# The opening loads of a fused attention and MLP kernel are regrouped, and its first input chunk is turned into eight half banks

## The chip, the cores and the metric

The kernel runs on one core of a Trainium2 chip. A core has a matrix engine (TensorE, PE in the profile), a vector engine (VectorE, DVE), an activation engine (ScalarE, ACT), a general engine (GpSimd, POOL) and SyncE (SP), which here only issues transfers. Each works through its own list of instructions in order, and waits on semaphores that other engines or transfers raise. Sixteen DMA engines move data between the device memory and the core's SBUF. Matrix products land in PSUM, which has eight banks of 128 partitions by 512 fp32 values.

The metric is device time in microseconds (us), lower is better. The kernel before takes 155.68 us, the median of three runs (155.62 to 155.93).

## The reference: what is computed

Inputs and output are bfloat16; `x` is 2048 by 512.

```python
x = A_x                                   # (1, 2048, 512)
g = sigmoid((x * gate_w).sum(-1, keepdims=True))
q, k, v = split heads of x @ wqkv         # 32 heads of 16
pq, pk = q @ w_phi[h], k @ w_phi[h]       # per head, 16 by 16
phi = concat(softmax(p), softmax(-p))     # 32 features, for q and for k
kv, z = phi_k^T v, sum of phi_k           # per head
o = (phi_q kv) / (phi_q z + 1e-6)
a = o @ wo
b = relu(x @ w1) @ w2                     # 512 -> 1376 -> 512
out = g * a + (1 - g) * b
```

## The kernel before, in words

**How the work is ordered.** Every piece of work is a task with a name, an engine, a list of tasks it depends on, an assumed duration and an assumed latency (`add`, lines 45 to 55). `schedule` (lines 94 to 121) places the tasks in time by a priority, tries random changes of the priorities, and keeps the order with the shortest plan; `emit` (lines 133 to 146) then writes each engine's list in that order, with a wait wherever a dependency crosses engines. So a change in a dependency or in an assumed number can move instructions on every engine.

**The opening.** All first loads are issued at once from two queues, SP and ACT (lines 287 to 295), with two small ones from POOL. `x0a` and `x0b` are the two halves of the first 512 rows of `x`; `wka` and `wkb` are the halves of the key weights; `w1a`, `w1b0`, `w1b1` and `w1c` are pieces of W1 and `wv` the value weights. While they are under way, TensorE runs eight dummy products (`warm`, line 262). Then, in this order:

- `xt`: the first chunk of `x` is turned by products with the identity, sixteen of 128 by 128 (line 342), into four PSUM banks; `xe` copies the turned chunk to SBUF, two copies on ACT (line 354) and two on DVE (line 357), each 128 by 512.
- `h0_0`, `h0_1`: the first two of eleven column tiles of `x @ w1` for chunk 0, four products each (line 397). Tile k of W1 covers columns 128k to 128k+127. `rl` is the ReLU behind each, on ACT.
- `wt`: the key weights are turned the same way (line 328) and copied out by `we`.
- `f1`: `w_phi` is folded into the key weights (line 372) and copied out by `fe1`. `f0` is the same for the query weights.
- `pr_k0` to `pr_k8`, `pr_q0` to `pr_q8`: the projections of two row tiles of 128 each (the last two of one) with the folded weights (line 468).
- `v0` to `v15`: the values of one row tile (line 448), copied out by `ve` on ACT; all of them use PSUM bank 2.

The other three chunks of `x` and the query weights come in through transposing transfers on the SP queue (lines 301 to 304). The first of them, `x1`, waits for `w1b1`, and the loads of W2 and Wo stand behind them on the same queue.

**The softmax chain.** For each projection J: `ev` (ACT) copies it to SBUF, `mx` and `mn` (DVE, lines 500 and 502) take the maximum and minimum of each head, `t1` and `t2` (POOL, line 509) subtract, `ex` (ACT, line 516) exponentiates, `sm` and `rc` (DVE) sum and invert, and `nm` (POOL, lines 525 and 548) scales. For the keys, `kv` (PE, line 532) then accumulates over all rows. For the queries, `tq` (SP, line 551) is a transposing transfer of one row tile, `nd` (PE, line 575) makes numerator and denominator in two halves, `rd` and `o` (DVE) divide, `to` (SP, line 588) is a transposing transfer of the result, and `a` (PE, line 602) multiplies it by Wo on top of `b` (PE, line 596), the eleven products with W2. `oe` (ACT) scales the sum and `st` stores it. All `tq` and `to` go through the one SP queue, in the planned order.

**The folds of the query weights.** `SP0` says behind which chunk of `h` the four folds `f0` stand in the chain that shares the PSUM banks 3, 4 and 5: with -1 behind chunk 1.

Of the kernel before, what the change touches and what calls it, by code (L numbers as in the profile page):

```python
# [6 lines left out]
ACT = mybir.ActivationFunctionType  # L7
# [141 lines left out]
def bass_gated_mix__linear_kernel_hedgehog__dense_activation_relu__prompt_kernel(  # L149
# [30 lines left out]
    NPB, NTS, NF, NSL = 3, 3, 4, 3  # L180
    NPH, NOM, NOT, NOS = 6, 3, 4, 4
    GATE_LIMIT = 40.0
    NWARM = 8
    RL = 400.0
    FE = "dve"
    SP0 = -1

    with ExitStack() as es:
        E = es.enter_context
# [4 lines left out]
        XT = sb("XT", [P, ND, S], BF16)  # L194
# [3 lines left out]
        WV = sb("WV", [P, ND, D], BF16)  # L198
        W1 = sb("W1", [P, ND, W1C], BF16)
# [22 lines left out]
        IDN = sb("IDN", [P, P], BF16)  # L222
# [9 lines left out]
        PS = E(nc.psum_tensor("PS", [P, 8, 512], FP32))  # L232
# [54 lines left out]
        load("x0a", "sp", XN[:, 0:2, :], x0r[:, 0:2, :], dur=0.5, lat=3.7)  # L287
        load("x0b", "act", XN[:, 2:4, :], x0r[:, 2:4, :], dur=0.5, lat=3.7)
        load("w1a", "sp", W1[:, :, 0:256], w1r[:, :, 0:256], dur=0.5, lat=5.5)
        load("wka", "act", WK[:, 0:2, :], wkr[:, 0:2, :], dur=0.5, lat=5.0)  # L290
        load("wkb", "sp", WK[:, 2:4, :], wkr[:, 2:4, :], dur=0.5, lat=5.8)
        load("w1b0", "act", W1[:, 0:2, 256:768], w1r[:, 0:2, 256:768], dur=0.5, lat=8.0)
        load("w1b1", "sp", W1[:, 2:4, 256:768], w1r[:, 2:4, 256:768], dur=0.5, lat=8.0)
        load("wv", "act", WV[:, :, :], A_wqkv[:, 2 * D:3 * D].rearrange("(j p) n -> p j n", p=P), dur=0.5, lat=11.1)
        load("w1c", "sp", W1[:, :, 768:DFF], w1r[:, :, 768:DFF], dur=0.5, lat=10.4)
        load("wphi", "pool", WPS[:, :, :], A_w_phi.rearrange("(g hl) r c -> (hl r) g c", g=ND), dur=0.9, lat=5.7)
        load("gw", "pool", W1[:, :, DFF:DFF + 1], gate_w.rearrange("(j p o) -> p j o", p=P, o=1), dur=0.8, lat=8.0,
             allow_slow_non_contiguous=True)
        g.follow("iota_r", "iota_i")
        g.follow("iota_i", "wphi")  # L300
        load_t("x1", XT[:, :, chunk(1)], x2[chunk(1), :], ("w1b1",), 2.6, 2.3)
        load_t("x2", XT[:, :, chunk(2)], x2[chunk(2), :], (), 2.0, 4.3)
        load_t("wqT", WT[:, 0:ND, :], A_wqkv[:, 0:D], (), 3.8, 2.3)
        load_t("x3", XT[:, :, chunk(3)], x2[chunk(3), :], (), 2.1, 2.2)
# [29 lines left out]
            else:  # L334
                add(name, eng, lambda q: q.tensor_copy(out_, PS[:, b, :]), deps, dur=0.69, **how)

        XB, WB, FB = (0, 1, 6, 7), (2, 6, 7, 0), (1, 2, 6, 7)

        def pe_xt(q, p, hf):
            for n in range(4):  # L340
                j, m = 2 * p + n // 2, 2 * hf + n % 2
                last = q.matmul(PS[:, XB[2 * hf + p], n * P:(n + 1) * P], XN[:, m, j * P:(j + 1) * P], IDN[:, :],
                                start=True, stop=True)
            return last

        for hf, ld in enumerate(("x0a", "x0b")):
            half = slice(hf * 256, (hf + 1) * 256)
            for p in range(2):
                add(f"xt{p}{hf}", "pe", lambda q, p=p, hf=hf: pe_xt(q, p, hf), (ld, "ident"), dur=0.32,
                    boost=9000.0 - 10 * (ND * hf + p))  # L350
                o3 = XT[:, 2 * p:2 * p + 2, half]
                i3 = PS[:, XB[2 * hf + p], :].rearrange("p (j t) -> p j t", j=2)
                if p == 0:
                    add(f"xe{p}{hf}", "act", lambda q, o=o3, i=i3: q.activation(o, i, ACT.Copy), (f"xt{p}{hf}",),  # L354
                        dur=0.6, boost=9000.0)
                else:
                    add(f"xe{p}{hf}", "dve", lambda q, o=o3, i=i3: q.tensor_copy(o, i), (f"xt{p}{hf}",), dur=0.69,  # L357
                        boost=9000.0)
        for i in range(ND):
            add(f"wt{i}", "pe", lambda q, i=i: pe_turn(q, WB[i], [WK[:, j, i * P:(i + 1) * P] for j in range(ND)]),  # L360
                ("wka", "wkb", "ident",
                *((f"xe{XB.index(WB[i]) % 2}{XB.index(WB[i]) // 2}",) if WB[i] in XB else ())), dur=0.28, boost=1900.0)
            evict(f"we{i}", ("act", "dve")[i % 2], WT[:, ND + i, :], WB[i], (f"wt{i}",), boost=1900.0)
        x0 = [f"xe{p}{hf}" for p in range(2) for hf in range(2)]
        xof = [x0, ["x1"], ["x2"], ["x3"]]
        wkt = [f"we{i}" for i in range(ND)]

# [78 lines left out]
        def pe_v(q, m):  # L446
            for j in range(ND):
                last = q.matmul(PS[:, 2, :], XT[:, j, m * P:(m + 1) * P], WV[:, j, :],  # L448
                                start=(j == 0), stop=(j == ND - 1))
# [24 lines left out]
        for jn, (kind, tiles) in enumerate(jobs):  # L474
# [15 lines left out]
            def old(x, J2=two):  # L490
# [1 line left out]

            add(f"pr_{J}", "pe", lambda q, s=s, tiles=tiles: pe_proj(q, s, tiles),
                [*(f"fe{s}_{j}" for j in range(ND)), *(d for m in tiles for d in xof[m // 4]),
                 *([f"ev_{before}"] if before else ["fe1_0", "we3"])], dur=0.87 * w)
            add(f"ev_{J}", "act", lambda q, pb=pb, w=w: q.activation(  # L496
                PB[:, pb, 0:w * D], PS[:, 0:w, :].rearrange("p a b -> p (a b)"), ACT.Copy),
                (f"pr_{J}", old("t1"), old("t2"), old("mx"), old("mn")), dur=0.15 + 0.43 * w)
# [11 lines left out]
                    (f"{'mx' if sg == 0 else 'mn'}_{J}", old("ex"), "warm"), dur=0.19 + 0.86 * w)  # L510
            war = [(f"kv{m}" if jobs[jn - NF][0] == "k" else f"tq{m}") for m in jobs[jn - NF][1]] if jn >= NF else []
            if jn == NF - 2:
                war += [f"xt{p}{hf}" for p in range(2) for hf in range(2)]
# [158 lines left out]
```

## Time and profile before

| | us |
|---|---|
| median of three runs | 155.68 |
| the profiled execution | 156.26 |
| its span | 154.5 |
| around the span | 1.8 |
| TensorE busy (936 products) | 147.5, 96% of the span |
| GpSimd busy | 111.1, 72% |
| VectorE busy | 113.8, 74% |
| ScalarE busy | 94.2, 61% |
| first projection `pr_k0` starts | 13.97 |
| first GpSimd subtraction `t1_k0` starts | 18.10 |

The profiled execution is 0.58 us above the median, so differences are read in it and applied to the median. The granted TensorE clock is given as 1.00 throughout. The chain of waits names 56% of the span for TensorE and 29% for GpSimd; both readings come from the same stretch, since between 10.3 and 99 us TensorE hardly rests while GpSimd is nearly as full.

### The profile page before, as it was taken

To read this page: it belongs to the slowest core of one execution; us is meant where nothing else is said; L and a number is where in the kernel's file an instruction comes from. 1 tells how busy PE (TensorE), PEld (TensorE's weight loads), DVE (VectorE), ACT (ScalarE), POOL (GpSimd) and SP (SyncE) were. 2 spreads that over 40 slices of the span, in tenths; PEclk is the share of its full clock that TensorE was granted. 3 is DMA by queue.
4 is the path that set the end of the run, shared out by engine and by line. 5 is a ranking of instruction groups with operands and counts; after the bars stand their busy time and mean duration, and the time that the engine had idled before them with its cause. 6 is when DMAs were issued, how large, how long until landed. Compare 5 with 4: busy or idle time off the path is not lost.

```text
span 154.5 us, 2461 instructions
## 1 busy us (share of the span) xinstructions
PE 147.5 (96%) x936; PEld 72.8 (47%) x936; DVE 113.8 (74%) x168; ACT 94.2 (61%) x127; POOL 111.1 (72%) x73
## 2 busy tenths in 40 slices
PE   6789999999999999999999999799999999999992
PEld 2455444554545644545454545344555445445440
DVE  3353668999986998489999777599789968934310
ACT  2366589969498959898997817386037712511123
POOL 8000396999999999999999999999786639530000
PEclk9999999999999999999999999999999999999999
DMA  4999999501000000000000061927569576697221
GB/s 138 268 345 234 117 240 311 173 1 1 6 0 0 0 5 0 2 0 0 5 0 0 0 136 34 147 63 170 149 157 143 145 192 159 148 162 178 72 68 68
DMA packets 43571, 15.59 MB, mean 101 GB/s; under 512 B 36532, under 2 KB 43556, under 8 KB 43560
## 3 DMA queue, kind: packets, MB, share of 16 engines
q1 hardware_dynamic: 39848, 12.01, 36.5%
q10 hardware_dynamic: 3648, 3.41, 7.6%
q0 software_dynamic: 64, 0.02, 0.4%
q8 instruction: 7, 0.11, 0.4%
q14 instruction: 4, 0.03, 0.1%
HBM read 4.94 MB, written 2.11 MB: 46 GB/s over the span
## 4 chain that ended last, share of the span: by engine, by line
PE 56%; POOL 29%; DMA 8%; issue 3%; ACT 1%; SPq 1%; ACTq 0%
PE PS L596 20%; POOL TS L509 15%; POOL FT L525 11%; PE PS L397 11%; PE PS L468 10%; PE PS L602 8%; DMA W<-in_B_w_dram 5%; PE PS L448 4%; DMA PHQ<-FT 3%; POOL FT L548 2%; PE PS L575 2%; SPq L272 1%; ACT OSB L609 1%; PE PS L532 1%; PE PS L372 1%
## 5 line engine op out<-in xcount | busy, mean ns | idle before, releaser
L397 PE MATMUL PS<-XT,W 128*128 128x512 bf16 (+1 forms) x176 | 41.4, 379 | 1.7 <-DVE XT L357 1.0
L509 POOL TENSOR_TENSOR TS<-PB,MX 128x1024 bf16<-128x1024 bf16 (+1 forms) x18 | 31.0, 1723 | 15.9 <-DVE MX L500 15.9
L518 DVE TENSOR_REDUCE ZB<-FT 128x128 f32<-128x2048 bf16 (+1 forms) x18 | 36.6, 2035 | 5.5 <-ACT FT L516 5.4
L596 PE MATMUL PS<-W,HT 128*128 128x512 bf16 (+1 forms) x176 | 40.6, 379 | 0.0
L516 ACT ACTIVATE FT<-TS 128x2048 bf16<-128x2048 bf16 (+1 forms) x18 | 30.9, 1716 | 11.7 <-POOL TS L509 11.7
L509 POOL TENSOR_TENSOR TS<-MN,PB 128x1024 bf16<-128x1024 bf16 (+1 forms) x18 | 31.0, 1724 | 1.9 <-DVE MN L502 1.9
L468 PE MATMUL PS<-WP,XT 128*128 128x512 bf16 x128 | 30.6, 379 | 0.0
L412 ACT ACTIVATE HT<-PS 128x512 bf16<-128x512 f32 (+1 forms) x44 | 25.9, 596 | 6.4 <-PE PS L397 5.8
L525 POOL TENSOR_TENSOR FT<-FT,SC 128x2048 bf16<-128x2048 bf16 (+1 forms) x9 | 29.5, 3285 | 0.0
L609 ACT ACTIVATE OSB<-PS,OMG 128x512 bf16<-128x512 f32 x16 | 11.0, 686 | 28.8 <-PE PS L602 28.8
L397 PEld LDWEIGHTS PS<-XT,W 128*128 128x128 bf16 (+1 forms) x176 | 17.2, 100 | 20.7 <-ACT XT L354 1.1
L596 PEld LDWEIGHTS PS<-W,HT 128*128 128x128 bf16 (+1 forms) x176 | 16.3, 98 | 17.7 <-ACT OSB L609 0.2
L500 DVE TENSOR_REDUCE MX<-PB 128x64 bf16<-128x1024 bf16 (+1 forms) x18 | 19.2, 1068 | 6.1 <-ACT PB L496 6.1
L502 DVE TENSOR_REDUCE MN<-PB 128x64 bf16<-128x1024 bf16 (+1 forms) x18 | 19.5, 1082 | 0.0
L496 ACT ACTIVATE PB<-PS 128x1024 bf16<-128x1024 f32 (+1 forms) x18 | 16.6, 923 | 4.6 <-PE PS L468 4.2
L468 PEld LDWEIGHTS PS<-WP,XT 128*128 128x128 bf16 x128 | 12.2, 98 | 13.9
L581 DVE RECIPROCAL RD<-PS 128x16 f32<-128x16 f32 x32 | 6.9, 239 | 14.3 <-PE PS L575 14.2
L448 PE MATMUL PS<-WV,XT 128*128 128x512 bf16 x64 | 16.4, 379 | 0.0
L602 PE MATMUL PS<-WO,OT 128*128 128x512 bf16 x64 | 16.1, 378 | 0.0
L548 POOL TENSOR_TENSOR FT<-FT,SR 128x1024 bf16<-128x1024 bf16 (+1 forms) x9 | 15.7, 1739 | 0.5
L583 DVE SCALAR_TENSOR_TENSOR OTM<-PS,EG,RD 128x256 bf16<-128x256 f32 x32 | 14.1, 463 | 0.1
L457 ACT ACTIVATE VS<-PS 128x512 bf16<-128x512 f32 x16 | 9.5, 595 | 2.6 <-PE PS L448 2.6
(47 smaller groups left out, 87.9 us busy)
## 6 DMA issues: line engine op xcount, KB each, us to landing
out_dram<-OSB ACTq DMA_DIRECT2D x16, 128.0 KB, 1.7
W<-in_B_w_dram SPq DMA_DIRECT2D x1, 1280.0 KB, 7.7
W<-in_B_w_dram SPq DMA_DIRECT2D x1, 608.0 KB, 10.2
W<-in_B_w_dram SPq DMA_DIRECT2D x2, 256.0 KB, 6.6
WV<-in_A_wqkv_dram ACTq DMA_DIRECT2D x1, 512.0 KB, 10.6
WO<-in_A_wo_dram SPq DMA_DIRECT2D x1, 512.0 KB, 7.8
FT<-in_A_x_dram SPq DMA_DIRECT2D x1, 256.0 KB, 3.3
FT<-in_A_x_dram ACTq DMA_DIRECT2D x1, 256.0 KB, 3.6
```

The source lines that it names most:

```text
L397: last = q.matmul(PS[0:m, b, :], W1[:, j, k * P:k * P + m], XT[:, j, chunk(c)], start=(j == 0), stop=(j == ND - 1))
L412: add(f"rl{a}_{k}", "act", lambda q, a=a, k=k, b=b, rows=rows: q.activation(HT[0:rows, k, chunk(a)], PS[0:rows, b, :], ACT.Relu), (prev,), ...
L448: last = q.matmul(PS[:, 2, :], XT[:, j, m * P:(m + 1) * P], WV[:, j, :], start=(j == 0), stop=(j == ND - 1))
L468: last = q.matmul(PS[:, n, :], XT[:, j, m * P:(m + 1) * P], WP[:, s, j, :], start=(j == 0), stop=(j == ND - 1))
L500: add(f"mx_{J}", "dve", lambda q, sl=sl, w=w, i=pbg: q.tensor_reduce(MX[:, sl, 0:w * H], i, AX.X, ALU.max), (f"ev_{J}", old("t1")), dur=0. ...
L502: add(f"mn_{J}", "dve", lambda q, sl=sl, w=w, i=pbg: q.tensor_reduce(MN[:, sl, 0:w * H], i, AX.X, ALU.min), (f"ev_{J}", old("t2")), dur=0. ...
L509: add(f"{tn}_{J}", "pool", lambda q, o3=o3, a3=a3, b3=b3: q.tensor_tensor(o3, a3, b3, ALU.subtract), (f"{'mx' if sg == 0 else 'mn'}_{J}", ...
L516: add(f"ex_{J}", "act", lambda q, fs=fs, ts=ts, w=w: q.activation(FT[:, fs, 0:w * F], TS[:, ts, 0:w * F], ACT.Exp), (f"t1_{J}", f"t2_{J}", ...
L518: add(f"sm_{J}", "dve", lambda q, fs=fs, sl=sl, w=w: q.tensor_reduce(ZB[:, sl, 0:2 * w * H], FT[:, fs, 0:w * F].rearrange("p (g d) -> p g ...
L525: add(f"nm_{J}", "pool", lambda q, f3=f3, sl=sl, w=w: q.tensor_tensor(f3, f3, SC[:, sl, 0:2 * w * H].unsqueeze(2).to_broadcast([P, 2 * w * ...
L596: last = q.matmul(PS[:, ab, :], HT[0:r, k, m * P:(m + 1) * P], W2[0:r, k, :], start=(k == 0), stop=False)
L602: last = q.matmul(PS[:, ab, :], OT[:, m % NOT, t, :], WO[:, t, :], start=False, stop=(t == ND - 1))
```

## The change

The nine first loads become nine others. `x0a` and `x0b` stay. W1's first 512 columns (tiles 0 to 3) come next, as two halves by rows, one on each queue (`w1a0`, `w1a1`), in place of 256 columns on SP. The key weights follow as halves `wk0` and `wk1`. Then come the other 864 columns of W1, again in halves (`w1b0`, `w1b1`), and `wv` last, on SP in place of ACT. The transfer `x1` waits for the new `w1b0`.

The turn of chunk 0 is cut from four groups of four products into eight groups of two, each into the first half of a bank of its own, so that all eight banks are used. There are eight copies of 128 by 256 in place of four of 128 by 512. The banks of `wt`, `f1` and the dependencies that protect them are renamed to match. The dummy products go from eight to seven, and `SP0` from -1 to -2, which puts the four folds `f0` behind chunk 2 of `h`.

The plan that comes out has on TensorE, up to the first projection: seven dummies, sixteen `xt`, `h0_0`, `h0_1`, `wt`, `h0_2`, `h0_3`, `f1`, `v0`, `h0_4`, `pr_k0`. Before, it was: eight dummies, `xt`, `h0_0`, `h0_1`, `wt`, `h0_2`, `f1`, `h0_3`, `h0_4`, `pr_k0`, `v0`. From there to `nd2` the same tasks stand in a somewhat other order on every engine.

```diff
-    NWARM = 8
+    NWARM = 7
-    SP0 = -1
+    SP0 = -2
...
-        load("w1a", "sp", W1[:, :, 0:256], w1r[:, :, 0:256], dur=0.5, lat=5.5)
-        load("wka", "act", WK[:, 0:2, :], wkr[:, 0:2, :], dur=0.5, lat=5.0)
-        load("wkb", "sp", WK[:, 2:4, :], wkr[:, 2:4, :], dur=0.5, lat=5.8)
-        load("w1b0", "act", W1[:, 0:2, 256:768], w1r[:, 0:2, 256:768], dur=0.5, lat=8.0)
-        load("w1b1", "sp", W1[:, 2:4, 256:768], w1r[:, 2:4, 256:768], dur=0.5, lat=8.0)
-        load("wv", "act", WV[:, :, :], A_wqkv[:, 2 * D:3 * D].rearrange("(j p) n -> p j n", p=P), dur=0.5, lat=11.1)
-        load("w1c", "sp", W1[:, :, 768:DFF], w1r[:, :, 768:DFF], dur=0.5, lat=10.4)
+        wvr = A_wqkv[:, 2 * D:3 * D].rearrange("(j p) n -> p j n", p=P)
+        qs = ("sp", "act")
+        for n, q in enumerate(qs):
+            load("x0" + "ab"[n], q, XN[:, 2 * n:2 * n + 2, :], x0r[:, 2 * n:2 * n + 2, :], dur=0.5, lat=3.7)
+        for name, dst, src, lat in (("w1a", W1[:, :, 0:512], w1r[:, :, 0:512], 4.8), ("wk", WK, wkr, 5.9),
+                                    ("w1b", W1[:, :, 512:DFF], w1r[:, :, 512:DFF], 8.0)):
+            for n, q in enumerate(qs):
+                load(f"{name}{n}", q, dst[:, 2 * n:2 * n + 2, :], src[:, 2 * n:2 * n + 2, :], dur=0.5, lat=lat)
+        load("wv", "sp", WV[:, :, :], wvr, dur=0.5, lat=9.0)
...
-        load_t("x1", XT[:, :, chunk(1)], x2[chunk(1), :], ("w1b1",), 2.6, 2.3)
+        load_t("x1", XT[:, :, chunk(1)], x2[chunk(1), :], ("w1b0",), 2.6, 2.3)
...
-        XB, WB, FB = (0, 1, 6, 7), (2, 6, 7, 0), (1, 2, 6, 7)
+        XB, WB, FB = (0, 1, 6, 7, 2, 3, 4, 5), (0, 1, 6, 7), (0, 1, 6, 7)
-        def pe_xt(q, p, hf):
-            for n in range(4):
-                j, m = 2 * p + n // 2, 2 * hf + n % 2
+        def pe_xt(q, j, hf):
+            for n in range(2):
+                last = q.matmul(PS[:, XB[4 * hf + j], n * P:(n + 1) * P], XN[:, 2 * hf + n, j * P:(j + 1) * P],
+                                IDN[:, :], start=True, stop=True)
...
+            for j in range(ND):
+                add(f"xt{j}{hf}", "pe", lambda q, j=j, hf=hf: pe_xt(q, j, hf), (ld, "ident"), dur=0.2,
+                    boost=9000.0 - 10 * (ND * hf + j))
+                xo, xi = XT[:, j, half], PS[:, XB[4 * hf + j], 0:256]
+                if j % 2 == 0:
+                    add(f"xe{j}{hf}", "act", lambda q, o=xo, i=xi: q.activation(o, i, ACT.Copy), (f"xt{j}{hf}",),
+                        dur=0.35, boost=9000.0)
                 else:
+                    add(f"xe{j}{hf}", "dve", lambda q, o=xo, i=xi: q.tensor_copy(o, i), (f"xt{j}{hf}",), dur=0.37,
                         boost=9000.0)
...
-            war = ["xe10"] if j == 0 else [f"we{j - 1}"]
+            war = [f"we{j}"]
...
-        freed = {b: () for b in HB}
-        w1of = {k: (("w1a",) if k < 2 else ("w1b0", "w1b1") if k < 6 else ("w1c",)) for k in range(KT)}
+        freed = {b: (f"xe{XB.index(b) % 4}{XB.index(b) // 4}",) for b in HB}
+        w1of = {k: (("w1a0", "w1a1") if k < 4 else ("w1b0", "w1b1")) for k in range(KT)}
...
-            add(f"v{m}", "pe", lambda q, m=m: pe_v(q, m), (*xof[m // 4], "wv", f"ve{m - 1}" if m else "fe1_1"), dur=0.87)
+            add(f"v{m}", "pe", lambda q, m=m: pe_v(q, m), (*xof[m // 4], "wv", f"ve{m - 1}" if m else "xe01"), dur=0.87)
...
-                 *([f"ev_{before}"] if before else ["fe1_0", "we3"])], dur=0.87 * w)
+                 *([f"ev_{before}"] if before else ["fe1_0", "fe1_1"])], dur=0.87 * w)
```

More of the change, by code (lines that the diff above doesn't have):

```diff
@@ L286, in bass_gated_mix__linear_kernel_hedgehog__dense_activation_relu__prompt_kernel @@
         wkr = A_wqkv[:, D:2 * D].rearrange("(j p) n -> p j n", p=P)
-        load("x0a", "sp", XN[:, 0:2, :], x0r[:, 0:2, :], dur=0.5, lat=3.7)
-        load("x0b", "act", XN[:, 2:4, :], x0r[:, 2:4, :], dur=0.5, lat=3.7)
-        load("w1a", "sp", W1[:, :, 0:256], w1r[:, :, 0:256], dur=0.5, lat=5.5)
-        load("wka", "act", WK[:, 0:2, :], wkr[:, 0:2, :], dur=0.5, lat=5.0)
-        load("wkb", "sp", WK[:, 2:4, :], wkr[:, 2:4, :], dur=0.5, lat=5.8)
-        load("w1b0", "act", W1[:, 0:2, 256:768], w1r[:, 0:2, 256:768], dur=0.5, lat=8.0)
-        load("w1b1", "sp", W1[:, 2:4, 256:768], w1r[:, 2:4, 256:768], dur=0.5, lat=8.0)
-        load("wv", "act", WV[:, :, :], A_wqkv[:, 2 * D:3 * D].rearrange("(j p) n -> p j n", p=P), dur=0.5, lat=11.1)
-        load("w1c", "sp", W1[:, :, 768:DFF], w1r[:, :, 768:DFF], dur=0.5, lat=10.4)
+        wvr = A_wqkv[:, 2 * D:3 * D].rearrange("(j p) n -> p j n", p=P)
[7 more added lines that the diff above has]
+        load("wv", "sp", WV[:, :, :], wvr, dur=0.5, lat=9.0)
         load("wphi", "pool", WPS[:, :, :], A_w_phi.rearrange("(g hl) r c -> (hl r) g c", g=ND), dur=0.9, lat=5.7)
@@ L335, in evict @@
                 add(name, eng, lambda q: q.tensor_copy(out_, PS[:, b, :]), deps, dur=0.69, **how)
-        XB, WB, FB = (0, 1, 6, 7), (2, 6, 7, 0), (1, 2, 6, 7)
-        def pe_xt(q, p, hf):
-            for n in range(4):
-                j, m = 2 * p + n // 2, 2 * hf + n % 2
-                last = q.matmul(PS[:, XB[2 * hf + p], n * P:(n + 1) * P], XN[:, m, j * P:(j + 1) * P], IDN[:, :],
-                                start=True, stop=True)
+        XB, WB, FB = (0, 1, 6, 7, 2, 3, 4, 5), (0, 1, 6, 7), (0, 1, 6, 7)
[3 more added lines that the diff above has]
+                                IDN[:, :], start=True, stop=True)
             return last
@@ L347, in bass_gated_mix__linear_kernel_hedgehog__dense_activation_relu__prompt_kernel @@
             half = slice(hf * 256, (hf + 1) * 256)
[L348 to L355, printed above, removed]
+            for j in range(ND):
[5 more added lines that the diff above has]
+                        dur=0.35, boost=9000.0)
                 else:
-                    add(f"xe{p}{hf}", "dve", lambda q, o=o3, i=i3: q.tensor_copy(o, i), (f"xt{p}{hf}",), dur=0.69,
+                    add(f"xe{j}{hf}", "dve", lambda q, o=xo, i=xi: q.tensor_copy(o, i), (f"xt{j}{hf}",), dur=0.37,
                         boost=9000.0)
@@ L360, in bass_gated_mix__linear_kernel_hedgehog__dense_activation_relu__prompt_kernel @@
             add(f"wt{i}", "pe", lambda q, i=i: pe_turn(q, WB[i], [WK[:, j, i * P:(i + 1) * P] for j in range(ND)]),
-                ("wka", "wkb", "ident",
-                *((f"xe{XB.index(WB[i]) % 2}{XB.index(WB[i]) // 2}",) if WB[i] in XB else ())), dur=0.28, boost=1900.0)
+                ("wk0", "wk1", "ident",
+                f"xe{i}0"), dur=0.28, boost=1900.0)
             evict(f"we{i}", ("act", "dve")[i % 2], WT[:, ND + i, :], WB[i], (f"wt{i}",), boost=1900.0)
-        x0 = [f"xe{p}{hf}" for p in range(2) for hf in range(2)]
+        x0 = [f"xe{j}{hf}" for j in range(ND) for hf in range(2)]
         xof = [x0, ["x1"], ["x2"], ["x3"]]
@@ L512, in bass_gated_mix__linear_kernel_hedgehog__dense_activation_relu__prompt_kernel @@
             if jn == NF - 2:
-                war += [f"xt{p}{hf}" for p in range(2) for hf in range(2)]
+                war += [f"xt{j}{hf}" for j in range(ND) for hf in range(2)]
             if jn == NF - 1:
```

## The prediction

> **What bounds the kernel now.** I read the busy shares first, then the chain of waits in order of time, then the waits, then the landings of the first loads, and last the transfers around the one gap in TensorE's work.
>
> ```profile
> PE 147.5 (96%) x936; PEld 72.8 (47%) x936; DVE 113.8 (74%) x168; ACT 94.2 (61%) x127; POOL 111.1 (72%) x73
> ```
>
> TensorE is the bound: 7.0 us of the span are all it does not fill. The chain says where those are:
>
> ```profile
> 2.30 7.89 DMA W<-in_B_w_dram
> 10.19 0.14 issue
> 10.33 1.02 PE PS L397 x4
> 11.35 0.89 PE PS L372 x16
> 12.24 1.73 PE PS L397 x8
> 13.97 1.73 PE PS L468 x8
> 15.70 0.86 PE PS L448 x4
> ...
> 95.62 4.50 DMA PHQ<-FT
> 100.12 0.05 issue
> 100.16 0.30 PE PS L575 x4
> ```
>
> `w1b1`, issued at 2.30, lands at 10.19 and releases `h0_2`. From there TensorE has no gap until 99.15, where it waits 1.0 us for `tq2`. The waits name the same places:
>
> ```profile
> ACT XT L354 <- PE PS L342: 1.1, 1, 1.1
> ...
> PE PS L575 <- DMA PHQ<-FT: 1.0, 1, 1.0
> PE PS L397 <- DVE XT L357: 1.0, 1, 1.0
> ...
> PE PS L397 <- DMA W<-in_B_w_dram: 0.7, 1, 0.7
> ```
>
> So three waits of TensorE can be won: 1.0 us for the copies of the turned `x` (until 6.84), 0.7 us for W1, and 1.0 us for `tq2`. The first loads, with the time from issue to landing at the end:
>
> ```profile
> W<-in_B_w_dram SPq DMA_DIRECT2D x1, 608.0 KB, 10.2
> ...
> WV<-in_A_wqkv_dram ACTq DMA_DIRECT2D x1, 512.0 KB, 10.6
> ...
> FT<-in_A_wqkv_dram SPq DMA_DIRECT2D x1, 256.0 KB, 6.3
> W<-in_B_w_dram ACTq DMA_DIRECT2D x1, 256.0 KB, 7.7
> ```
>
> With their issues (2.78, 2.35, 1.76, 1.80) they land at 13.0, 12.95, 8.1 and 9.5. Meanwhile the DMA engines moved this much per microsecond (last column, GB/s):
>
> ```profile
> 7.00:8.00 1.00, 1.00 (x6) 0.47 (x5) 0.51 (x3) 0.10 (x1) 0.00 (x0) 1.00 0.79 110
> ...
> 9.00:10.00 1.00, 0.62 (x12) 0.44 (x8) 1.00 (x2) 1.00 (x3) 0.00 (x0) 1.00 1.09 384
> ```
>
> The last row to see is the transfers between 97.5 and 98.2 us:
>
> ```profile
> q1 hardware_dynamic: 413, 0.10, 64.0%
> q8 instruction: 1, 0.02, 10.8%
> ```
>
> A single instruction load of 16 KB runs while `tq2` does. `tq2` took 4.5 us to land, its neighbours `tq0` and `tq1` 2.7 and 2.8. With 2.8 it would have been there at 98.4, before TensorE asked at 99.15: the 1.0 us gap hangs on that coincidence.
>
> **The opening, step by step.** I call the start of `pr_k0` P0; it is 13.97 before.
>
> Turning `x`: the eight dummies run at 0.43 us each from 1.19, so with seven the turn starts about 4.2 instead of 4.58 (`x0a` lands at 0.74 + 3.3 = 4.0, `x0b` at 0.75 + 3.6 = 4.4, both in time). A copy of 512 columns takes 0.59 on ACT and 0.69 on DVE. One of 256 is not in the trace: half of that at least, the whole at most. ACT's 1024 columns take 1.02 (line 496), 0.43 more than 512, so 256 should take 0.59 - 0.21 = 0.38; for DVE I take 0.37. Four on ACT from 4.95 (two groups of two products at the slow 0.11 us each, then 0.25 us) end at 6.5, and `h0_0` starts at 6.6 instead of 6.84 (bounds 6.2 and 7.3). `w1a0` and `w1a1` lie behind as many bytes as `w1a` (6.46) and `wka` (6.3) did: covered, barely. One dummy less is less work for TensorE before: if the faster pace of products, seen from about 5.0 us on, came later, `h0_0` and `h0_1` would run at 0.43 instead of 0.216 each, 1.7 us more; the turn follows at once, so I give that little.
>
> `h0_0` and `h0_1`: 1.73, to 8.4. `wt` needs `wk0` and `wk1`, third on their queues. The third on SP landed at 8.1 before, the third on ACT at 9.5; I take 8.8, between, since the bytes ahead on ACT are the same but SP no longer moves 512-byte rows. So `wt` waits 0.4 (0 to 1.1), and then 0.14 + 0.89 for `wt`, 1.73 for `h0_2` and `h0_3` (their W1 is long there; the 0.7 us wait is gone) and 0.89 for `f1`: 12.45.
>
> Next in order is `v0`, and it needs `wv`, now the last load. The bytes are the same 2,912 KB. Early bound: the rates by the microsecond sum to 2.71 MB at 11.0, the remaining 0.27 MB pass by 11.9. Late bound: SP now carries 1,712 KB instead of 1,632; 80 KB at 270 KB/us (W2 and Wo, 1,888 KB from 23.65 to 30.65) behind 13.0 is 13.3. I take 12.6, since W1 in longer rows and a wait of `x1` for later bytes both leave the engines freer. Then 0.14 + 1.02 (a first group after a wait, as at 10.33) and 0.86 for `h0_4`: P0 = 14.6 (14.0 to 15.3).
>
> The Trainium skill, DMA: Bandwidth & Descriptors, section Issuing engines are not separate DMA queues, says that transfers started from several engines run on the same 16 DMA engines, and that this saves issue time only. By that the same bytes end when they did, at 13.0, P0 is 15.0 and the sum below 0.4 us higher. The trace agrees so far: `wv` on ACT and `w1c` on SP landed within 0.05 us of each other.
>
> So TensorE has done `v0` (0.86) more when it reaches `pr_k0`, 0.65 later. GpSimd, which waits for `pr_k0`, starts 0.65 later too, at 18.75.
>
> **From P0 to `nd2`.** TensorE's tasks from P0 to `nd2` in the new order: 13 projections of 1.73, two of 0.86, 15 `v` and 39 `h` of 0.86, `kv` 4.1, `f0` 0.9, three `b` of 2.38, `a0` 0.86, four `nd` of 0.13: 84.3 us. Before it was 85.1 (with `v0`), and 13.97 + 85.1 = 99.1 is what the trace shows. GpSimd's tasks up to `nm_q1` are the same set in another order: it ended at 94.84, P0 + 80.9. That keeps the one gap of 1.73 at `t1_k2`, whose tasks stand in the same order. Against these sums, `kv` comes at least 0.8 us behind its `nm` (0.4 before), `t1` at least 2.4 behind its projection: no new wait. Cover that is gone: `f0` moves from 49 to about 62, and `pr_q0`, once 10 us behind, follows `f0_3` with only 1.6 us of TensorE work between, while two copies of 0.69 and 0.25 us stand on DVE. I take 0.1, bounds 0 and 0.7, hidden as long as `nd2` waits anyway. `x1` is issued at about 11 instead of 10.2, and everything behind it on SP shifts by that; `x1` then lands at 16 and is wanted at 21.5, W2 at 30 and 88.
>
> `tq2` is issued behind `nm_q1` and `to0`, both at P0 + 80.9. TensorE reaches the tenth product of `b2`, where the instruction load came, at P0 + 83.1, 2.2 us later; before it was 97.87 - 95.62 = 2.25. So if the load is tied to TensorE's place in its list, it meets `tq2` again, whatever P0 is: `nd2` starts at P0 + 80.95 + 4.5 = 100.1 instead of 100.16.
>
> **The end.** The tasks behind `nd2` are the same, 50.8 us. Before, `a15` waited 0.2 us for `to15`; now `a13` stands between `nd15` and `b15`, so `to15` is 0.9 us earlier: -0.2. DVE's and GpSimd's other order there touches transfers with slack, `to3` and `to5` with almost none.
>
> Sum: -0.06 - 0.2 = -0.26. In the profiled execution 156.26 becomes 156.0; the median is 0.58 lower, so 155.4.
>
> **The rivals.** About 0.2% (0.3 us) is what a measurement of this kernel can tell from no change.
>
> First: `tq2` and the instruction load miss each other. The load met only the end of `tq2`, so 0.2 us of shift is enough. Then `nd2` starts at P0 + 84.3 = 98.9, -1.26, and -0.2 at the end: 154.2; `to3` (needed about 0.2 us after it lands) and `to5` (0.0) may take back up to 0.4. The Trainium skill, Runtime: NRT & Kernel Launch, section Instruction fetch mechanics, has instructions refilled in 16 KiB blocks and calls the cost mostly hidden; the block size agrees with the 0.02 MB here, the cost does not. By the page the wait would not return.
>
> Second, the other side: `wv` decides. As the last load it lands with the last byte, 13.0 as `w1c` did, up to 13.3, and everything waits for it, GpSimd's whole chain included. P0 is 15.0 to 15.3, `nd2` 100.5 to 100.8, the time 155.8 to 156.2; from 13.2 on it is slower than before by more than 0.3. For it: equal bytes, an equal end. Against: fewer short rows, and SP alone reached 374 GB/s at 26 us. A straggler like `tq2`'s among `wv`'s pieces would add 1.7: 157.
>
> Third: the loads are early (`wk` at 8.1, `wv` at 12.0). P0 is 14.0, and with the wait at `nd2` the time 154.8. For it: the windows' 350 to 384 GB/s around 9 us. Against: 110 GB/s between 7 and 8, which the small gate load at that time would repeat.
>
> Fourth: a new wait in the rearranged middle or tail (`pr_q0`, `to5`, or another transpose met by an instruction load, 1.0 to 1.7), 156.5.
>
> **How the numbers follow.** The forecast, 0.38, range 154.9 to 155.9: I put 0.15 on faster, 0.20 on the same, 0.03 on slower. First rival 0.26: 0.25 faster, 0.01 the same. Second 0.17: 0.13 slower, 0.04 the same. Third 0.07: faster. Fourth 0.12: slower. Together: faster 0.47, same 0.25, slower 0.28. The range leaves out the early loads without the wait and a straggler: 154.0 to 156.5.
>
> **What would show it.** In the profile after: `h0_0` near 6.6; no wait of line 395 for W1 in front of `h0_2`; a wait of `v0` (line 446) for `wv` that ends at 12.6; `pr_k0` at 14.6, `t1_k0` at 18.75; `nd2` at 100.1 with a `tq2` of 4.5 us and an instruction packet beside it. The prediction is wrong if `pr_k0` starts before 14 or after 15.3, if `nd2` finds `tq2` landed, or if TensorE shows a gap over 0.3 us elsewhere.

## The result, and the profile after

The changed kernel takes 157.03 us where the kernel before takes 155.91 beside it: 1.0071 times as long, 95% interval 1.0043 to 1.0100. Three of the seven executions of the changed kernel, at 159.1 to 159.3 us with a granted clock of 0.989, belong to a slower state and are left out; the median of all seven is 157.44. A second measurement gave 157.35 us against 155.50, 1.0110 (1.0081 to 1.0139). It is slower by about 1%; the forecast was 0.2% faster.

The profiled execution of the changed kernel took 156.53 us (span 154.6). It is the shortest of the changed kernel's executions, while that of the kernel before (156.26) was among the longest of its own, so the two lie closer than the medians. TensorE remains the bound:

```profile
PE 147.0 (95%) x935; PEld 72.6 (47%) x935; DVE 113.7 (74%) x170; ACT 94.4 (61%) x129; POOL 111.0 (72%) x73
```

The chain of waits of the changed kernel in order of time (start, us, what), at the three places that the prediction spoke of:

```profile
1.79 7.52 DMA FT<-in_A_wqkv_dram
9.31 0.14 issue
9.44 1.05 PE PS L328 x16
10.50 1.73 PE PS L395 x8
12.22 0.89 PE PS L370 x16
13.12 0.86 PE PS L446 x4
13.98 0.86 PE PS L395 x4
14.84 1.73 PE PS L466 x8
...
98.60 0.86 PE PS L600 x4
99.47 0.25 PE PS L573 x8
...
111.58 2.15 DVE ZB L516
113.73 0.27 DVE OTM L581
113.99 0.04 issue
114.03 0.11 DVE SC L540
114.14 3.95 DMA OT<-OTM
118.09 0.04 issue
118.14 1.04 PE PS L600 x4
```

Opening: the second half of the key weights lands at 9.31 and releases `wt`; `v0` follows `f1` without a wait; `pr_k0` starts at 14.84 with `v0` already done. Middle: `nd2` follows `a0` at 99.47 without a wait. Tail: `a5` waits for `to5`, which was issued at 114.14 behind `o5_1`, itself behind `sm_q4` (2.15 us), and took 3.95 us to land. TensorE's waits (total, times, longest) say the same:

```profile
PE PS L328 <- DMA FT<-in_A_wqkv_dram: 1.3, 1, 1.3
PE PS L259 <- DVE TS L255: 1.2, 1, 1.2
PE PS L395 <- DMA W<-in_B_w_dram: 1.0, 1, 1.0
PE PS L600 <- DMA OT<-OTM: 0.8, 1, 0.8
```

The transfers of the changed kernel from 116 to 118.2 us hold, as in the window that the prediction showed, one load of 16 KB of instructions, this time beside `to5`:

```profile
q8 instruction: 1, 0.02, 2.5%
```

Compared with the earlier profile: up to `pr_k0` TensorE has the same work done at the same time (14.84 less the 0.86 of `v0` is 13.98; before 13.97), at `nd2` it is 0.69 ahead (99.47 for 100.16), and from there to `a14`, the last group of products but one, it takes 50.18 us where it took 49.36: it loses 0.82.

### The profile page after: what moved, and what is told of

Its sections match the earlier page's. It is cut to its first block, busy times and chain, and to the rows that moved or that the text cites. A ratio compares the mean times of both kernels' runs of the same rounds, so it can differ in the third digit from the quotient of the medians.

```text
span 154.6 us, 2474 instructions
## 1 busy us (share of the span) xinstructions
PE 147.0 (95%) x935; PEld 72.6 (47%) x935; DVE 113.7 (74%) x170; ACT 94.4 (61%) x129; POOL 111.0 (72%) x73
## 4 chain that ended last, share of the span: by engine, by line
PE 85%; DMA 7%; ACT 3%; DVE 2%; ACTq 1%; issue 0%
PE PS L395 22%; PE PS L594 22%; PE PS L466 18%; PE PS L446 9%; PE PS L600 8%; DMA FT<-in_A_wqkv_dram 5%; DMA OT<-OTM 3%; PE PS L530 3%; PE PS L573 2%; DVE ZB L516 1%; ACT FT L514 1%; PE PS L370 1%; ACT OSB L607 1%; ACT HT L410 1%; PE PS L328 1%; ACTq L272 1%
## 5 line engine op out<-in xcount | busy, mean ns | idle before, releaser
L581 DVE SCALAR_TENSOR_TENSOR OTM<-PS,EG,RD 128x256 bf16<-128x256 f32 x32 | 13.6, 457 | 0.0
```

## The experiments

The table is a key to them. For the profiled execution of nine kernels it gives the start of `pr_k0` and of `a14` by the chain, and the difference; where `v0` stands ahead of `pr_k0`, its 0.86 is taken off the start. In the kernels of one order the work between is the same.

| kernel | ratio to before (95%) | `pr_k0` | `a14` | between | TensorE's waits between |
|---|---|---|---|---|---|
| before | 1 | 13.97 | 149.52 | 135.55 | `nd2` 1.0 |
| before, 7 dummies | 0.9996 (0.9973 to 1.0018) | 13.87 | 148.82 | 134.95 | `nd3` 0.4 |
| loads only | 1.0059 (1.0035 to 1.0083) | 14.59 | 149.52 | 134.93 | `nd3` 0.4 |
| half banks only | 0.9989 (0.9972 to 1.0006) | 13.60 | 148.56 | 134.96 | `nd3` 0.4 |
| loads and half banks, order before | 1.0024 (1.0003 to 1.0046) | 14.97 | 150.15 | 135.18 | `nd2` 0.7 |
| changed kernel | 1.0071 (1.0043 to 1.0100) | 13.98 | 149.65 | 135.67 | `a5` 0.8 |
| changed kernel again | 1.0110 (1.0081 to 1.0139) | 13.99 | 150.58 | 136.59 | `nd2` 0.6, `a5` 1.0 |
| changed, tail of before | 1.0053 (1.0024 to 1.0082) | 14.51 | 149.60 | 135.09 | none |
| loads, half banks, tail of after | 1.0111 (1.0089 to 1.0134) | 14.53 | 150.88 | 136.35 | `a1` 0.7, `a5` 1.0 |

### Again, and the dummies

The changed kernel once more (no edit), the changed kernel with eight dummies, and the kernel before with seven:

```diff
-    NWARM = 7
+    NWARM = 8
```
```diff
-    NWARM = 8
+    NWARM = 7
```

> The changed kernel once more, beside the kernel before on one chip, for the spread of its executions and their granted clocks. Theory 1 (the opening waits for the key weights until 9.3 and P0 is 14.8; the end of the kernel moves only by what collides there): span near 154.6 to 155.0 and a ratio of 1.002 to 1.004. Theory 2 (something beside the profiled waits, such as a spell of half clock, is in most executions): ratio 1.006 to 1.010, and some executions with a mean granted clock of 0.99, that is one window of 3.4 us at half.

> The changed kernel with eight dummy products instead of seven, and the order of all other instructions as it is. Theory 2a (the missing dummy is what lets the clock come late or go back): granted clock 1.000 in every execution, time 0.5 to 1.5 us below the changed kernel. Theory 2b (the clock goes back because TensorE rests 1.0 us for W1 and 1.3 us for the key weights within one window): clock and time as in the changed kernel. Theory 1: the turn of x starts at 4.58 instead of 4.15, h0_0 at 6.6 instead of 6.3, and the key weights at 9.3 hide it: no difference, within 0.2 us.

> The kernel before with seven dummies instead of eight, same order. Theory 2a: some executions with a granted clock of 0.99, and the others slower by up to 0.5 us. Theory 2b: clock 1.000 throughout. Theory 1: the turn starts 0.3 us earlier, h0_0 at 6.5, and the wait for w1b1 (10.19) swallows it: within 0.2 us of before.

Measured: 157.35, 157.05 (ratio 1.0097, 1.0070 to 1.0124) and 155.51 us. The number of dummies moves neither kernel beyond the intervals. The ratio of the first, 1.0110, is far above its theory 1 and just above its theory 2, but the half clock that theory 2 thought of is not there: over the three kernels no execution had a mean granted clock under 0.996. And the wait for `to5` is in all three profiles of the changed order: 0.8, 1.0 and 1.2 us.

### The loads, the half banks, and both

All tasks that both kernels have stand in the order of the kernel before (a list of names per engine in place of the planner); only the loads are new:

```diff
+        for name, dst, src, lat in (("w1a", W1[:, :, 0:512], w1r[:, :, 0:512], 4.8), ("wk", WK, wkr, 5.9),
+                                    ("w1b", W1[:, :, 512:DFF], w1r[:, :, 512:DFF], 8.0)):
...
-        order = g.schedule()
+        order = {e: [g.tasks[n] for n in FIXED[e]] for e in ENGINES}
```

> The kernel before with the new first loads alone: the old turn of x, eight dummies, and the order of before on every engine (h0_2, f1, h0_3, h0_4, pr_k0, v0). Theory 1: wt waits for the key weights until 9.3 (8.56 before), h0_2 no longer waits, f1 waits about 0.8 us for the copies of wt, pr_k0 starts near 14.7 (13.97 before); TensorE and GpSimd are both 0.7 us later than before, so the time is 0.5 to 0.8 us above before. If the loads themselves are harmless, pr_k0 starts by 14.0 and the time is as before.

Measured: 156.57 us, ratio 1.0059: theory 1, though 0.1 us or more over its 0.5 to 0.8. The landing of the key weights takes the place of the landing of W1 as what holds TensorE. Its waits for `h0_0` (copies of `x`) and `wt` in this kernel:

```profile
PE PS L433 <- DVE XT L393: 0.8, 1, 0.8
PE PS L364 <- DMA FT<-in_A_wqkv_dram: 0.7, 1, 0.7
```

`pr_k0` is 0.62 to 0.72 later than in the two profiles of the order before, and everything behind it takes as long as it did (134.93). The wait of 0.8 us for the copies of `wt` that was expected at `f1` is not there: `h0_2` covers it.

The counterpart, half banks with the old loads, in the same order:

```diff
+        XB, WB, FB = (0, 1, 6, 7, 2, 3, 4, 5), (2, 6, 7, 0), (1, 2, 6, 7)
-        def pe_xt(q, p, hf):
+        def pe_xt(q, j, hf):
```

> The kernel before, its loads and its order on every engine, with x's first chunk turned into eight half banks and nothing else. Theory 1 (the halves only bring x's turn forward, and the next wait, h0_2 for its W1 columns at 10.3 us, takes it back): h0_0 starts near 6.4 us instead of 6.84, pr_k0 stays at 13.9 to 14.0, 155.3 to 155.7 us. Theory 2 (the halves' gain reaches the end): pr_k0 at 13.5, 155.0 to 155.2. Theory 3 (the halves are a cost, 16 evictions' fixed parts on ScalarE and VectorE): 155.9 or more.

Measured: 155.41 us for 155.44, ratio 0.9989. No cost, and no gain that the measurement can tell: `h0_0` goes from waiting for the copies to waiting for its W1 columns. `pr_k0` did come forward, to 13.60, which is nearer to theory 2, but the time is that of theory 1.

Both parts under the order before:

> Both parts of the change, loads and half banks, under the order of the kernel before on every engine (names of the turned blocks apart), so that only the new plan is left out. Theory 1 (the key weights' landing near 9.3 us sets the opening: wt 9.45, h0_2, f1, h0_3, h0_4 behind it, pr_k0 = 9.45+1.05+0.86+0.89+1.73 = 13.98): pr_k0 at 13.9 to 14.4, 155.5 to 156.0 us, and the changed kernel's other 1.4 us or so come from the plan. Theory 2 (the loads' loss of the run with the loads alone stays, the halves give nothing): pr_k0 at 14.5 to 14.7, 156.4 to 156.7.

Measured: 155.91 us for 155.44, ratio 1.0024. In the profiled execution the second half of the key weights landed at 1.81 + 8.32 = 10.13, the latest of all, in the chain of this kernel:

```profile
1.81 8.32 DMA FT<-in_A_wqkv_dram
```

So that execution (156.89) stands above its median and its `pr_k0` lies above both ranges, but the median keeps to theory 1. Loads and half banks cost 0.2% under the old order, the whole change 0.7 to 1.1%. The rest, 0.5 to 0.9%, is the new order.

### Exchanging the tails

From `b0` (TensorE), `t1_q3` (GpSimd), `ex_q2` (ScalarE), `rd0_0` (VectorE) and `tq0` (SyncE) to the end, both orders hold the same tasks, so the tails can be exchanged. In the changed kernel, and the same line with the other tail in the kernel with loads and half banks:

```diff
         order = g.schedule()
+        order = {e: [t for t in order[e] if t.name not in TAIL[e]] + [g.tasks[n] for n in TAIL[e]] for e in ENGINES}
```

> The changed kernel whose written order is, from b0 on TensorE, t1_q3 on GpSimd, ex_q2 on ScalarE, rd0_0 on VectorE and tq0 on SyncE to the end, that of the kernel before; its loads, its half banks and its order up to there (v0 ahead of pr_k0 too) stay. Theory 1 (what the new plan loses it loses in the tail, where a5 stands ahead of b7): no wait at a5, 155.7 to 156.3 us, 0.2 to 0.5% over the kernel before, as with loads and half banks under the order before (155.91). Theory 2 (the plan loses in the opening and the middle): 156.9 to 157.5 us, as the changed kernel.

> The counterpart: loads and half banks under the order before (155.91 us), with the changed plan's order from b0, t1_q3, ex_q2, rd0_0 and tq0 on. Theory 1 (the tail is the loss): TensorE waits 0.8 to 1.2 us for to5 at a5, 156.7 to 157.4 us. Theory 2 (it is not): 155.7 to 156.2 us.

Measured: 156.47 us for 155.70 (1.0053) with the tail of before; 157.39 (1.0111) with the tail of after. TensorE's waits in the first, which has none behind the opening:

```profile
PE PS L347 <- DMA FT<-in_A_wqkv_dram: 1.5, 1, 1.5
PE PS L278 <- DVE TS L274: 1.2, 1, 1.2
PE PS L414 <- ACT XT L371: 0.5, 1, 0.5
```

and in the second, with `a5` and one more transpose of the tail:

```profile
PE PS L655 <- DMA OT<-OTM: 1.6, 2, 1.0
PE PS L383 <- DMA FT<-in_A_wqkv_dram: 1.5, 1, 1.5
```

The tail of after adds 0.87% to the kernel that had 1.0024, and those two intervals lie well apart. Taking it out of the changed kernel brings 1.0071 and 1.0110 down to 1.0053: the same way, but the interval of 1.0053 overlaps the first in most of its width and just touches the second. So theory 1 is shown by the second exchange and agrees with the first. The first of them stayed 0.2 us over its range: its key weights landed at 9.83, 0.5 later than in the changed kernel's own profile.

### Why `to5`, and why not before

The trace of the kernel before already held it. Its `to5`, in the view of its line in a narrow window (start, and the time from issue to landing):

```profile
L588 SPq DMA_TRANSPOSE OT<-OTM x1: 1217/1217/1217, 115.5 to 115.5; - x1
...
DMA to landing us min/median/max: 4.5/4.5/4.5
```

It too landed late, at 120.0, with an instruction load beside it from 117.9 to 118.9. But `a5` stood behind `b7`, 2.4 us of matmuls that need no transpose, and came at 120.8. The new plan has `a5` ahead of `b7`, and TensorE comes to it at 117.3.

Over the 18 profiles of this case I set the landing of every transpose beside the instruction loads. A transpose into `OT` during whose usual 2.3 us such a load of 16 KB began landed 3.7 us after its issue in the median (53 of them, 36 at 3.5 or more). Without one it took 2.3, with an output store beside it (171, one at 3.5) and without (44, none); 20 that met a load earlier or later, many of them late too, are left out. That goes together; it does not show a cause yet. First, the transpose was moved:

```diff
+        ahead("dve", ["o5_1"], "sm_q4")
+        ahead("sp", ["to4", "to5"], "tq7")
```

> The changed kernel with one pair of moves in its written order: on VectorE o5_1 stands ahead of sm_q4 (2.15 us), and on SyncE to4 and to5 stand ahead of tq7, so that to5 is issued near 112.3 us and not at 114.1. All else is the changed kernel. Theory 1 (TensorE's wait of 0.85 to 1.2 us for to5 at a5 is a loss of its own, beside the opening): the wait goes, a5 starts right behind nd7_0, and the time falls from 157.35 us by 0.8 to 1.2, to 156.1 to 156.6, about what the new loads alone gave (156.57). Theory 2 (the opening is the whole loss, and a later wait takes whatever a5 gains): 157.1 to 157.5, with a new TensorE wait of 0.7 us or more behind 118 us.

Measured: 157.08 us, ratio 1.0086 (1.0060 to 1.0113). `to4` and `to5` now landed in their usual time, and the next in the queue, `tq7`, was caught instead. Two views of this kernel, `to4` and `to5`, then `tq7`, and TensorE's wait:

```profile
L586 SPq DMA_TRANSPOSE OT<-OTM x2: 1210/1228/1247, 111.7 to 113.0; - x2
...
DMA to landing us min/median/max: 2.4/2.4/2.5
```
```profile
L549 SPq DMA_TRANSPOSE PHQ<-FT x1: 1302/1302/1302, 114.3 to 114.3; - x1
...
DMA to landing us min/median/max: 4.6/4.6/4.6
```
```profile
PE PS L573 <- DMA PHQ<-FT: 1.1, 1, 1.1
```

The load came at 115.4 to 116.9, the wait for `to5` became one of 1.1 us for `nd7`, and the time hardly moved. That is the later wait of theory 2; that the opening be the whole loss is not shown by it, and the exchange of the tails speaks against it. `to5` itself is not slow there; what is in flight around 116 is.

Then the load was to be moved, by 60 empty instructions at the head of TensorE's list, in the changed kernel and in the kernel with loads, half banks and `h0_2` in the gap (below):

```diff
+            for _ in range(60):
+                q.nop()
             g.emit("pe", q, order, sems)
```

> The changed kernel with 60 instructions that do nothing at the head of TensorE's list. A load of 16 KB of instructions came in every profile of the changed plan at 116.0 to 116.8 us and again 21 us after the one near 95, so some 12.5 of TensorE's instructions pass in a us, and 60 more should bring each load forward by about 4.8 us, that one to 111 to 112. Theory 1 (to5 lands 3.95 to 4.26 us after its issue, and not 2.4 to 2.9, because this load is under way): to5 lands in under 3 us, a5's wait of 0.85 to 1.2 falls below 0.3, the transposes of 110 to 112 are late instead, with more slack (nd7 at 117); 156.2 to 156.8 us. Theory 2 (to5 is late because three transposes and an output store go out together there): to5 and a5's wait as they were, 157.0 to 157.5.

> The run with loads, half banks and h0_2 in the gap, under the order before, with the same 60 empty instructions at the head of TensorE's list. There the instruction load at 97.9 us lay on tq3 (issued 96.81, 4.55 us to land) and nd3 waited 0.4 us. Theory 1 (the load's place sets which transpose is late): the load moves to 93 to 93.5 us, tq3 lands in under 3 us and the wait of 0.4 goes, 154.8 to 155.1 us, below the kernel before. Theory 2 (tq3 is late for another reason): the wait stays, 155.3 to 155.5.

Measured: 156.84 us (1.0081, 1.0050 to 1.0111) and 155.33 us (0.9986, 0.9962 to 1.0010). In the first the load did not move: 116.2, for 116.0 to 116.8 without them. The chain there has `to5` late as ever:

```profile
114.53 3.84 DMA OT<-OTM
```

In the second the load of 97.9 came at 94.6, those of 116.9 and 134.4 stayed within 0.4; a shift of one load of that size is also seen between two executions of the changed kernel itself (100.0 and 95.3). But neither trace has a row of the 60 instructions: the changed kernel's holds 2474 with them and without. So these two runs do not tell whether the loads follow the count of TensorE's instructions; what sets their time is open. Neither changed the time by more than its interval.

The load near 97 us moves by itself, though, and the late transpose moves with it. Ten of the profiled kernels issue their transposes in the order of before throughout. In seven of them the load came at 97.6 to 98.6; in three (the kernel before with the cover below, loads and half banks, and the filled gap with the empty instructions) it came at 94.6 to 96.1. Time from issue to landing in us:

| | load at | `to0` | `tq3` |
|---|---|---|---|
| order before, seven profiles | 97.6 to 98.6 | 2.3 | 4.0 to 4.7 |
| order before, three profiles | 94.6 to 96.1 | 3.2 to 3.6 | 2.8 to 2.9 |
| changed kernel, first profile | 100.0 | 2.3 | 2.8 |
| changed kernel, second profile | 95.3 | 3.5 | 2.8 |

The last two rows are one kernel without an edit. So at this place it is the load beside it, and not the transpose or its place in the queue, that goes with the late landing. For `to5` the trace cannot part the two: a load came beside it in every profile in which it was issued at its place.

Last, the transposes were covered in the kernel with `to5` early:

```diff
+        ahead("pe", ["a4", "a5", "b7"], "nd7_0")
+        ahead("pe", ["a7"], "a8")
+        ahead("dve", ["rc_q5", "mn_q6", "mx_q7"], "rd7_1")
```

> The run with to4 and to5 issued early, where the transpose of tq7 came 4.60 us after its issue and nd7 waited 1.1 us, with b7 (2.4 us of matmuls that need no transpose) moved ahead of both nd7, behind a4 and a5; a7 stands right ahead of a8, and on VectorE rc_q5, mn_q6 and mx_q7 ahead of rd7_1, so that nothing queues behind the later nd7. Theory 1 (the plan's loss is that no long matmul stands ahead of the work that needs the transpose then in flight; the order before had b7 ahead of a5): no TensorE wait over 0.3 us between 110 and 130 us, and 0.8 to 1.1 us less than without: 156.0 to 156.3. Theory 2 (the wait moves on to a further transpose, as it moved from to5 to tq7): a new wait of 0.5 us or more, 156.8 to 157.2.

Measured: 157.89 us, 1.0150 (1.0121 to 1.0180): worse, and above both ranges. The wait at `nd7` went, and a new one of 1.2 us came at 126.44, for a `tq10` that had landed in its usual time:

```profile
123.51 2.88 DMA PHQ<-FT
```

My own move of `a7` behind `nd10_0` had taken away what stood ahead of it. This run shows how little slack that tail has; it neither supports nor refutes the cover. The 0.8 us by which it is longer than the run before it is not fully placed.

### Work into the gap, and a cover that holds

In the kernel with both parts under the order before, `h0_2` was moved into TensorE's wait for the key weights (and `h0_3` between `wt` and `f1`):

```diff
-h0_0 h0_1 wt3 wt2 wt0 wt1 h0_2 f1_2 f1_1 f1_3 f1_0 h0_3 h0_4
+h0_0 h0_1 h0_2 wt3 wt2 wt0 wt1 h0_3 f1_2 f1_1 f1_3 f1_0 h0_4
```

> As the run with loads and half banks under the order before, and h0_2 ahead of the four wt (0.86 us of work, its W1 columns already there, into TensorE's wait for the key weights), h0_3 between wt and f1; on ScalarE rl0_2 and rl0_3 move with them. Theory 1 (TensorE's wait of about 1 us for the key weights is lost time that this work fills): pr_k0 at 13.1 to 13.6, and 0.4 to 0.9 us less than the run without the move: 154.7 to 155.3 us, below the kernel before. Theory 2 (a shorter opening is taken back by GpSimd's list or by a transpose later): the same as without the move within 0.2 us.

Measured: 155.39 us, 0.9994 (0.9977 to 1.0010), 0.5 us below the run without the move: the cost of the loads is gone. `pr_k0` came at 13.70, 0.1 above the range; the time too is just above it, and the kernel before isn't beaten.

Under the order before, one wait for a transpose with an instruction load beside it is left in most profiles: `nd3`, for `tq3`, 0.4 us. Two moves cover it, first in the kernel with half banks alone, then in the kernel before, then with the loads and the filled gap:

```diff
+        ahead("pe", ["b3"], "nd3_0")
+        ahead("dve", ["o2_1", "sm_q3"], "rd3_0")
```

> The run with the half banks alone (155.41 us), where the instruction load at 97.7 us lay on tq3 and nd3 waited 0.4 us for it: b3, 2.4 us of matmuls that need no transpose, moves ahead of nd3_0 on TensorE, and o2_1 and sm_q3 ahead of rd3_0 on VectorE. Theory 1 (a transpose that an instruction load delays costs only what TensorE has not to do meanwhile): the wait of 0.4 goes and nothing comes in its place, 154.9 to 155.2 us, 0.2 to 0.4% below the kernel before. Theory 2 (the gain is given back at a later wait, as in both earlier moves): 155.3 to 155.6 us.

> The kernel before with only the two moves that took the wait of nd3 away in the run with the half banks (154.88 us): b3 ahead of nd3_0 on TensorE, o2_1 and sm_q3 ahead of rd3_0 on VectorE. Theory 1 (the covered transpose is the gain, the half banks give nothing): 154.9 to 155.3 us, 0.2 to 0.4% below the kernel before. Theory 2 (the half banks are needed for it, since they bring pr_k0 0.3 us forward): 155.4 to 155.7 us.

> The loads and half banks of the change, h0_2 in TensorE's wait for the key weights, the order before for the rest, and the same two moves of b3, o2_1 and sm_q3. Theory 1 (the loads cost nothing once their gap is filled, and the cover pays here too): 154.8 to 155.1 us, as the run with the half banks and the cover. Theory 2 (the later key weights still cost): 155.3 to 155.7 us.

Measured: 154.88 us for 155.70 (0.9956, 0.9929 to 0.9984), 155.16 for 155.50 (0.9966, 0.9948 to 0.9983) and 154.82 for 155.50 (0.9958, 0.9941 to 0.9974). TensorE's waits in the first of them, all:

```profile
PE PS L431 <- DMA W<-in_B_w_dram: 1.6, 2, 1.2
PE PS L295 <- DVE TS L291: 1.2, 1, 1.2
```

`tq3` there still took 4.7 us to land, with an instruction load from 98.4 to 99.4 beside it, and nobody waits. Theory 1 holds in all three: the kernel before with the cover alone is 0.34% faster. (In that kernel's own profile the load came early, at 95.4, and `tq3` landed in 2.9, so its profile does not show the cover at work; the other two do.) The three intervals overlap, so nothing can be said of what half banks or loads add to it; but with the gap filled and the transpose covered, the loads of the change cost nothing. These three beat both kernels.

## Why the prediction was wrong, by its own steps

Two of the three signs it gave of being wrong came: `nd2` found `tq2` landed, and TensorE showed a gap of 0.8 us elsewhere, at `a5`.

- **The turn of `x`.** `h0_0` at 6.6, bounds 6.2 and 7.3. It started at 6.29; in two more profiles of the changed order at 6.54 and 6.97. The time is right. In the first profile what ended the wait were the W1 columns (1.0 us), which it had called covered, barely; in the other two it was the copies.
- **The key weights.** Taken at 8.8, bounds 8.1 and 9.5, "between" the third load of SP and that of ACT. Mis-sized: 9.31 in the first profile, and 9.31 to 10.13 over the profiles of kernels with these loads. Both halves are needed, so ACT's, the later row (9.5), was the one to take, not the middle. The row for 7 to 8 us was shown and then used only against the early rival; it came back, with 104 GB/s (the last column) for 110. That this stretch is what made the key weights late is not shown:

```profile
7.00:8.00 1.00, 1.00 (x6) 0.33 (x4) 0.00 (x0) 0.60 (x1) 0.00 (x0) 1.00 0.73 104
```

- **`wv`.** Forecast 12.6, landed at 2.77 + 9.87 = 12.64. Right, but it decided nothing: with `wt` half a us late, TensorE came to `v0` at 13.12, not at 12.45. The rule from the Trainium skill (DMA: Bandwidth & Descriptors, section Issuing engines are not separate DMA queues), that transfers share the same engines whoever starts them, would have put the end of the same bytes at 13.0; the trace has it 0.4 earlier. Over the profiles of kernels with these loads it lies between 12.29 and 13.21, so neither number is told from the other.
- **P0.** 14.6, bounds 14.0 and 15.3; 14.84. Inside, by luck: `wt`, `h0_2`, `h0_3` and `f1` ended 0.7 later than forecast, and the wait of `v0` for `wv` was not there. GpSimd started at 18.97 for 18.75.
- **`nd2`.** This step failed. It had `tq2` meet the instruction load again, "if the load is tied to TensorE's place in its list". In the profile `tq2` landed unhindered and `nd2` started at 99.47; in the second profile a load at 95.3 came beside `to0`, whose issue took 2.4 us on SP for 1.2, so `tq2` was issued 1.2 us later and `nd2` waited 0.6. One kernel, and the load of the middle at 100.0 and at 95.3: the condition does not hold for this load. In this one place the first rival was what the first profile showed.
- **The base.** I noted that the profiled execution lay 0.58 above the median, without asking what was in it. Its wait of 1.0 at `nd2` was; the same order with seven dummies showed 0.4 at `nd3`, and 135.55 against 134.95 from `pr_k0` to `a14`. So a wait of 1.0 was counted on both sides of the sum, where the other profiles of the order before, as far as no cover was put in, have 0.3 to 0.7.
- **The end.** The step that failed, and the one that decided the sign. "The tasks behind `nd2` are the same, 50.8 us", less 0.2: the tasks were the same, their order was not. `to5` was named there as having almost no slack, and then given no price in the sum; its landing was taken as usual although the trace before already had it at 4.5 us, covered by `b7`. With `a5` ahead of `b7` TensorE waited 0.7 to 1.2 us for it in every profile of the changed order that left it in place. The 0.2 was worth nothing. `a15` does start earlier behind `a14`, its wait for `to15` being gone (150.38 for 150.41, with `a14` 0.13 later). But ScalarE's `oe15` starts 0.5 us behind the end of `oe14` in both kernels, once `st14` has been issued, at 151.58 before and 151.72 after. The chain of the changed kernel runs through `a14`, `oe14`, the issue of `st14` and `oe15`:

```profile
149.65 0.88 PE PS L600 x4
...
150.56 0.70 ACT OSB L607
...
151.27 0.34 ACTq L610
...
151.72 0.69 ACT OSB L607
```

So where 0.2 was to be won from `nd2` to the end, 0.8 was lost. This is the fourth rival (0.12): its mechanism, its place and its time of 156.5 are what the first profile shows; the median of 157.03 is 0.5 above that, and that of the second measurement 0.9.
- **What is not placed.** From the profile of the order before with seven dummies (155.60 us) to the second of the changed kernel (157.45), `a14` is 1.76 later. `pr_k0` accounts for 0.12, the waits at `a5` and for `PHQ` for 1.2. Of the other 0.4, TensorE's weight load waits 0.3 for ScalarE (a copy of line 410, near 87 us) in each of the first three profiles of the changed order and not in the one with seven dummies; what is left is spread too thin to name.

## What to carry to other kernels

A late transfer that nobody waits for is invisible in the waits: before an order is changed, list the transfers that land late but covered, and see what the new order puts behind them. When an edit goes through a planner, hold the order fixed to price the edit, and exchange parts of the order to price the plan; here the edit cost 0.2% and the plan the rest. A wait for a load is cheapest filled with work whose data are already there, and work that needs no transfer belongs ahead of work that needs a late one.

## What was unexpected of the hardware

Transposes in flight when a 16 KB instruction load starts land late: 3.7 us in the median for 2.3, up to 4.9. The move of `to5` out of its way, after which `tq7` was caught, and the load near 97 that shifts by itself and changes which transpose is late, support the load as the cause. No edit moved a load, so it is not shown by taking it away. The Trainium skill (Runtime: NRT & Kernel Launch, section Instruction fetch mechanics) calls the cost of these refills mostly hidden; whether that is so for the engine that fetches no run here tells, but the transposes beside them landed 1.3 us later in the median. There were seven such loads in each profile. Most came at nearly the same place in every execution of an order; one came at 95.3 to 95.9 in three profiles of the changed plan and at 100.0 to 101.6 in three others, and of the three with the early load two waited at `nd2` (0.6 and 0.2 us), of the others none.

The second half of the key weights, a load of 256 KB behind `x` and 512 columns of W1, landed anywhere from 9.3 to 10.1 us in kernels with the same loads: 0.8 us of spread in the first 10 us, passed on to TensorE in full wherever no work was put into the gap.
